# One output store on one DMA ring in place of two stores on two rings, at the end of a load-bound decode kernel

## The chip, the cores and the metric

The kernel runs on one core of a Trainium2 chip. The metric is the device time of one execution in microseconds (us). Most executions agree within 0.3%. Beside the time, a profile gives the span, from the first to the last instruction; the time is about 1.8 us longer than the span.

Engines are called by their names in the profile: PE is TensorE's matmuls and PEld its weight loads, DVE is VectorE, ACT is ScalarE, SP is SyncE. "SPq" and "ACTq" are the sequencers of SyncE and ScalarE where they issue DMA transfers. SyncE's transfers go over queue q1, ScalarE's over q10. In this text such a queue is called a ring.

## The reference

A decode step for 8 sequences: a layer norm, attention of 32 query heads over the last 2,048 positions of a cache with 8 key and value heads, an output projection, and a two-layer perceptron with GELU. Cut to what matters:

```
h  = x + attention(layernorm(x), k_cache[:, :, -2048:], v_cache[:, :, -2048:], wq, wo)
b  = layernorm(h)
x1 = b                      # the token-shift branch is zero for one token
out = h + x1 + gelu(layernorm(x1) @ w3) @ w4        # out: 8 x 1 x 512, bf16
```

The two caches' windows are 67 MB of the 79 MB that must be read. The output is only 8 KB.

## The kernel before

SyncE issues every load: the input, the weights wq, 64 key tiles and 64 value tiles of 512 KB, then wo, w3 and w4. TensorE transposes the keys, does the products, and at the end accumulates the output in one PSUM bank: columns 0 to 255 of the result in partitions 0 to 7, columns 256 to 511 in partitions 32 to 39. The code places the two halves in two column tiles (its tile_position); in the trace of before, the two matmuls of a chunk of w4 start 2 to 6 ns apart.

```
NQ = 2
DQ = D // NQ                                    # 256
out_sb = sb([128, DQ], dt.bfloat16, "out_sb")
fin_ps = b6[:, 0:DQ]                            # fp32, PSUM

W4_CUT = [0, 8, 14]                             # w4 comes in two parts
def sp_prog(e):
    e.dma_start(x_sb[:], A_x...).then_inc(sem_x, 16)
    e.dma_start(wq_v, A_wq...).then_inc(sem_wq, 16)
    # ... 64 key tiles, 64 value tiles, wo, w3, w4: all issued here ...
    store_out(e, 0)
    e.wait_ge(sem_out, 16 * NQ)

def store_out(e, j):
    e.wait_ge(sem_dveP, DVEP_OUT_READY)
    e.dma_start(out.rearrange("b s d -> (b s) d")[:, j * DQ:(j + 1) * DQ],
                out_sb[32 * j:32 * j + B, :]).then_inc(sem_out, 16)

def pe_fin(e):
    # ... residual first, then, for each of the 14 chunks fc of w4 and j in 0, 1:
    #     waits for the part of w4 that fc begins
    #     fin_ps[32*j : 32*j+8, :] += gT[:, chunk fc]^T @ w4_sb[:, fc, half j]

def dve_final(e):
    e.wait_ge(sem_peP, PEP_FIN)
    e.tensor_copy(out_sb[0:40, :], fin_ps[0:40, :]).then_inc(sem_dveP, 1)   # 32*(NQ-1)+B = 40

AC.append(lambda e: store_out(e, 1))            # ScalarE issues the second half
```

Of the kernel before, what the change touches and what calls it, by code (L numbers as in the profile page):

```python
# [6 lines left out]
dt = mybir.dt  # L7
ACT = mybir.ActivationFunctionType
# [3 lines left out]
B = 8  # L12
D = 512
# [20 lines left out]
def bass_sequential_preLN__sliding_block_cached__mixer_s_mlp__decode_kernel(  # L34
# [23 lines left out]
    with es:  # L58
        sb = lambda shape, dtype, name: es.enter_context(nc.sbuf_tensor(name, shape, dtype))
# [69 lines left out]
        gT = sb([128, FC * B], dt.bfloat16, "gT")  # L129
        NQ = 2  # L130
        DQ = D // NQ
        out_sb = sb([128, DQ], dt.bfloat16, "out_sb")

        kT_ps = [ps_t([128, W], dt.bfloat16, f"kT_ps{i}") for i in range(2)]
        S_ps = ps_t([128, 2, 512], dt.float32, "S_ps")
# [16 lines left out]
        sem_out = S("sem_out")  # L152
# [27 lines left out]
        sem_peP = S("sem_peP")  # L180
        sem_dveP = S("sem_dveP")
        sem_actP = S("sem_actP")
# [19 lines left out]
        ev_act = Ev(sem_actP)  # L202
# [26 lines left out]
        def sp_prog(e):  # L229
            e.dma_start(x_sb[:], A_x.rearrange("b s d -> (b s) d")).then_inc(sem_x, 16)  # L230
            e.dma_start(wq_v, A_wq.rearrange("(p k) n -> p k n", k=KC)).then_inc(sem_wq, 16)  # L231
            v_next = 0

            def issue_v(i):
                b, g = divmod(i, G)
                vs = i % NV
                if i >= NV:
                    e.wait_ge(sem_PV, (i - NV) // G + 1)
                e.dma_start(  # L239
                    vnat[:, vs, :].rearrange("p (c d) -> p c d", c=NC),  # L240
                    A_v_cache[b, g, W0:SK, :].rearrange("(p c) d -> p c d", c=NC),
                ).then_inc(sem_v[vs], 16)

            for i in range(NITEM):
                b, g = divmod(i, G)
                ks = i % NK
                if i >= NK:
                    e.wait_ge(sem_Thi, i - NK + 1)
                e.dma_start(  # L249
                    knat[:, ks, :].rearrange("p (c d) -> p c d", c=NC),  # L250
                    A_k_cache[b, g, W0:SK, :].rearrange("(p c) d -> p c d", c=NC),
                ).then_inc(sem_k[ks], 16)
                while v_next <= i - VD and v_next < V_DEFER_FROM:
                    issue_v(v_next)
                    v_next += 1

            def issue_wo(j):
                h0, h1 = WO_CUT[j], WO_CUT[j + 1]
                e.dma_start(wo_v[:, h0:h1, :],  # L259
                            A_wo[h0 * 128:h1 * 128, :].rearrange(  # L260
                                "(h p) n -> p h n", p=128)).then_inc(sem_wo[j], 16)

            e.wait_ge(sem_dveP, DVEP_QBLK)
            wo_next = 0
            while v_next < NITEM:
                if NITEM - v_next == G // 2:
                    while wo_next < WO_EARLY:
                        issue_wo(wo_next)
                        wo_next += 1
                issue_v(v_next)  # L270
                v_next += 1
            while wo_next < WO_PARTS:
                issue_wo(wo_next)
                wo_next += 1
            if W34_LAST_ITEM >= 0:
                e.wait_ge(sem_Thi, W34_LAST_ITEM + 1)
            e.dma_start(w3_sb, B_w3.rearrange("(k p) f -> p k f", k=KC)).then_inc(sem_w3, 16)  # L277
            w4_rows = B_w4.rearrange("(c p j) n -> p c (j n)", p=128, j=2)
            w4_dst = w4_sb.rearrange("p (c j) n -> p c (j n)", j=2)
            for i in range(W4_PARTS):  # L280
                c0, c1 = W4_CUT[i] // 2, W4_CUT[i + 1] // 2
                e.dma_start(w4_dst[:, c0:c1, :], w4_rows[:, c0:c1, :]).then_inc(sem_w4[i], 16)
            store_out(e, 0)
            e.wait_ge(sem_out, 16 * NQ)

        def store_out(e, j):
            e.wait_ge(sem_dveP, DVEP_OUT_READY)
            e.dma_start(out.rearrange("b s d -> (b s) d")[:, j * DQ:(j + 1) * DQ],
                        out_sb[32 * j:32 * j + B, :]).then_inc(sem_out, 16)

        PE, AC, DV = [], [], []

# [286 lines left out]
        fin_ps = b6[:, 0:DQ]  # L579
# [96 lines left out]
        PEP_FIN = ev_pe.next()  # L676
# [22 lines left out]

        def dve_final(e):  # L700
            e.wait_ge(sem_peP, PEP_FIN)
            e.tensor_copy(out_sb[0:32 * (NQ - 1) + B, :], fin_ps[0:32 * (NQ - 1) + B, :]).then_inc(sem_dveP, 1)  # L702
        DV.append(dve_final)

        AC.append(lambda e: store_out(e, 1))

        with nc.Block() as block:
            block.gpsimd(pool_prog)
            block.sync(sp_prog)

            @block.tensor
            def _(e):
                for f in PE:
                    f(e)

            @block.scalar
            def _(e):
                for f in AC:
                    f(e)

            @block.vector
            def _(e):
                for f in DV:
                    f(e)
# [28 lines left out]
```

## Time and profile before

| | before |
|---|---|
| time, median of 4 runs | 207.62 us (207.40 to 207.75) |
| time and span of the profiled run | 207.02 us, 205.2 us |
| bytes over the DMA queues | 79.59 MB, 388 GB/s on average |
| last matmul's end to end of span | 2.3 us, 1.1% of the span |

The first two parts of the profile page of the kernel before follow: busy time, then tenths of busy time in 40 equal slices of the span. PEclk is the granted TensorE clock in tenths of full speed.

```profile
PE 159.2 (78%) x2744; PEld 122.6 (60%) x2744; DVE 83.5 (41%) x197; ACT 81.4 (40%) x100; POOL 3.0 (1%) x13
...
PE   1039975999599967995799878797998698875745
...
PEclk9999999797979799979995998599859797675557
DMA  6999999999999999999999999999999999999980
```

The DMA row is at nine tenths or more in all but the first slice and the last two. The load stream is what lasts; PE is busy for 78% but rarely in a full row. The chain of waits of the same kernel, by engine, says so too:

```profile
DMA 53%; SPq 31%; PE 13%; issue 2%; DVE 0%
```

VectorE has 0% of that chain and ScalarE nothing. Now the end, in the timeline of the kernel before. Columns: start in us, duration in us, engine, line, operation, output and inputs, and in brackets the idle time before it.

```profile
200.06 2.85 PE L692 MATMUL b<-knat,gT 128*8 128x256 bf16 x28 [0.51 <-DMA knat<-in_B_w_dram]
201.89 0.73 PEld L692 LDWEIGHTS b<-knat,gT 128*8 128x8 bf16 x12 [0.46 <-DMA knat<-in_B_w_dram]
202.96 0.42 DVE L702 CAST out_sb<-b 40x256 bf16<-40x256 f32 x1 [5.85 <-PE b L692]
203.40 0.32 SPq L288 DMA_DIRECT2D out_dram<-out_sb  x1
203.41 0.65 ACTq L288 DMA_DIRECT2D out_dram<-out_sb  x1
```

The last group of matmuls waits 0.51 us for the first part of w4, then runs without a gap. One copy of 0.42 us follows, then two issues that start together: SyncE's takes 0.32 us, ScalarE's 0.65 us. What SyncE waits for at the end of the kernel before:

```profile
SPq L707 <- DMA out_dram<-out_sb: 1.1, 1, 1.1
SPq L707 <- PEq L707: 0.2, 1, 0.2
```

That is 1.1 us for the stores to land and 0.2 us for the closing barrier. When the stores' packets move is seen in the DMA view cut to windows. Columns: packets, MB, share of the window on 16 engines. First 203.9 to 204.3 us, then 204.3 to 204.5 us of the kernel before:

```profile
q1 hardware_dynamic: 16, 0.00, 4.5%
...
q10 hardware_dynamic: 16, 0.00, 9.0%
```

SyncE's 16 packets (8 rows of 512 bytes, and 8 of 4 bytes, which stand for the updates of the semaphore) are all over before the first of ScalarE's 16 starts.

### The profile page before, as it was taken

Reading aid. Unit: us, or ns where it says so; the run is one execution under the profiler, and the core shown is the slowest. Engines: PE = TensorE matmul, PEld = TensorE weight load, DVE = VectorE, ACT = ScalarE, POOL = GpSimd, SP = SyncE. Lnnn points to the kernel's source line nnn. Section 1 sums busy time; section 2 is a strip of 40 time slices with the busy share of each in tenths; the row PEclk is TensorE's granted clock in tenths of the full one; section 3 lists DMA queues with packets and bytes.
Section 4 is the critical chain, followed back from the end, with each engine's and each line's share of the span. In section 5 each row is a group of like instructions: output and inputs, shape, how many; then the busy total and the mean of one; then the engine's idle time right before and its main releaser. Section 6 shows DMA issues by size and latency. Waiting matters only on the chain.

```text
span 205.2 us, 6281 instructions
## 1 busy us (share of the span) xinstructions
PE 159.2 (78%) x2744; PEld 122.6 (60%) x2744; DVE 83.5 (41%) x197; ACT 81.4 (40%) x100; POOL 3.0 (1%) x13
## 2 busy tenths in 40 slices
PE   1039975999599967995799878797998698875745
PEld 0039853697469654963487648574876476554632
DVE  5103544544453446343543554346435353352130
ACT  3203656515541554153513551176135431350040
POOL 5000000000000000000000000000000000000000
PEclk9999999797979799979995998599859797675557
DMA  6999999999999999999999999999999999999980
GB/s 206 434 398 415 409 407 409 407 411 408 403 410 406 408 410 410 406 406 410 409 410 405 409 411 410 407 406 410 406 409 408 407 410 385 359 394 328 394 334 28
DMA packets 24266, 79.59 MB, mean 388 GB/s; under 512 B 2200, under 2 KB 6320, under 8 KB 24112
## 3 DMA queue, kind: packets, MB, share of 16 engines
q1 hardware_dynamic: 24224, 79.19, 98.1%
q8 instruction: 22, 0.36, 0.7%
q14 instruction: 4, 0.03, 0.0%
q10 hardware_dynamic: 16, 0.00, 0.0%
HBM read 79.18 MB, written 0.01 MB: 386 GB/s over the span
## 4 chain that ended last, share of the span: by engine, by line
DMA 53%; SPq 31%; PE 13%; issue 2%; DVE 0%
DMA knat<-in_A_k_cache_dram 47%; SPq L239 17%; SPq L249 9%; PE kT_ps L388 6%; DMA knat<-in_B_w_dram 6%; SPq L259 4%; PE misc L526 3%; PE b L692 1%; PE S_ps L418 1%; SPq L277 1%; PE b L507 0%; DVE out_sb L702 0%; SPq L230 0%; SPq L231 0%; PE b L473 0%
## 5 line engine op out<-in xcount | busy, mean ns | idle before, releaser
L388 PE MATMUL kT_ps<-ident_b,knat 128*128 128x128 bf16 x1024 | 83.8, 248 | 21.7 <-DMA knat<-in_A_k_cache_dram 20.8
L399 ACT ACTIVATE kT_sb<-kT_ps 128x1024 bf16<-128x1024 bf16 x64 | 65.4, 1022 | 87.0 <-PE kT_ps L388 87.0
L388 PEld LDWEIGHTS kT_ps<-ident_b,knat 128*128 128x128 bf16 x1024 | 71.8, 113 | 38.6 <-DMA knat<-in_A_k_cache_dram 30.3
L406 DVE COPY kT_sb<-kT_ps 128x1024 bf16<-128x1024 bf16 x64 | 44.2, 691 | 62.8 <-PE kT_ps L388 62.8
L526 PE MATMUL misc<-pT_sb,vnat 128*128 128x4 bf16 x1024 | 29.0, 165 | 3.0 <-issue 1.4
L526 PEld LDWEIGHTS misc<-pT_sb,vnat 128*128 128x128 bf16 x1024 | 27.5, 98 | 6.1 <-issue 3.2
L418 PE MATMUL S_ps<-kT_sb,qblk 128*32 128x512 bf16 x256 | 29.0, 440 | 0.0
L418 PEld LDWEIGHTS S_ps<-kT_sb,qblk 128*32 128x32 bf16 x256 | 6.7, 94 | 9.0 <-issue 3.2
L439 ACT ACTIVATE P_sb<-S_ps,negmcol 128x512 bf16<-128x512 f32 x8 | 5.5, 687 | 7.7 <-DVE negmcol L431 7.6
L360 PE MATMUL S_ps<-xlnT,wbig 128*128 128x8 bf16 x128 | 3.6, 168 | 6.3 <-DMA wbig<-in_A_wq_dram 6.3
L536 DVE TENSOR_TENSOR prod_sb<-misc,w_sb 128x128 f32<-128x128 f32 x8 | 2.3, 292 | 14.6 <-PE misc L526 14.6
L512 DVE COPY w_sb<-b 128x128 f32<-128x128 f32 x8 | 2.3, 292 | 13.2 <-PE b L507 13.2
L360 PEld LDWEIGHTS S_ps<-xlnT,wbig 128*128 128x128 bf16 x128 | 3.5, 104 | 6.4 <-issue 6.4
L429 DVE TENSOR_REDUCE mcol<-S_ps 128x1 f32<-128x512 f32 x8 | 5.5, 682 | 0.6 <-PE S_ps L418 0.6
L584 ACT ACTIVATE std<-var,eps_t 128x8 f32<-128x8 f32 x1 | 0.3, 301 | 12.5 <-DVE var L635 12.5
L376 DVE TENSOR_SCALAR qblk<-S_ps 128x32 bf16<-128x32 f32 x8 | 0.9, 181 | 9.7 <-PE S_ps L360 9.7
L463 ACT ACTIVATE a_row<-d_row 1x128 f32<-1x128 f32 x8 | 2.4, 306 | 5.9 <-DVE d_row L456 5.9
L446 PE MATMUL misc<-ident_f,mcol 128*1 128x128 f32 x16 | 3.8, 328 | 1.0 <-DVE negmcol L431 1.0
L507 PE MATMUL b<-w_row,ones_row 1*128 1x128 f32 x16 | 4.2, 343 | 0.0
L602 PE MATMUL S_ps<-oT_all,wbig 128*128 128x8 bf16 x128 | 3.7, 168 | 0.5 <-DMA wbig<-in_A_wo_dram 0.5
L602 PEld LDWEIGHTS S_ps<-oT_all,wbig 128*128 128x128 bf16 x128 | 3.6, 104 | 0.6 <-DMA wbig<-in_A_wo_dram 0.6
L662 PE MATMUL misc<-uT,knat 128*128 128x8 bf16 x56 | 1.7, 168 | 2.7 <-DMA knat<-in_B_w_dram 2.7
(77 smaller groups left out, 68.6 us busy)
## 6 DMA issues: line engine op xcount, KB each, us to landing
knat<-in_A_k_cache_dram SPq DMA_DIRECT2D x64, 512.0 KB, 15.7
vnat<-in_A_v_cache_dram SPq DMA_DIRECT2D x64, 512.0 KB, 15.8
wbig<-in_A_wq_dram SPq DMA_DIRECT2D x1, 4096.0 KB, 12.2
wbig<-in_A_wo_dram SPq DMA_DIRECT2D x1, 2048.0 KB, 20.3
knat<-in_B_w_dram SPq DMA_DIRECT2D x1, 1792.0 KB, 12.1
wbig<-in_A_wo_dram SPq DMA_DIRECT2D x1, 1024.0 KB, 12.4
wbig<-in_A_wo_dram SPq DMA_DIRECT2D x2, 512.0 KB, 11.2
knat<-in_B_w_dram SPq DMA_DIRECT2D x1, 1024.0 KB, 12.6
```

Of the source, the lines that this page charges most:

```text
L239: e.dma_start(vnat[:, vs, :].rearrange("p (c d) -> p c d", c=NC), A_v_cache[b, g, W0:SK, :].rearrange("(p c) d -> p c d", c=NC),).then_inc ...
L249: e.dma_start(knat[:, ks, :].rearrange("p (c d) -> p c d", c=NC), A_k_cache[b, g, W0:SK, :].rearrange("(p c) d -> p c d", c=NC),).then_inc ...
L259: e.dma_start(wo_v[:, h0:h1, :], A_wo[h0 * 128:h1 * 128, :].rearrange("(h p) n -> p h n", p=128)).then_inc(sem_wo[j], 16)
L360: ins = e.matmul(S_ps[:, 0, h * B:(h + 1) * B], wq_v[:, kc, h * DH:(h + 1) * DH], xlnT[:, kc * B:(kc + 1) * B], start=(kc == 0), stop=(kc ...
L388: ins = e.matmul(buf[:, c * 128:(c + 1) * 128], knat[:, ks, c * DH:(c + 1) * DH], ident_b[:, :], is_transpose=True)
L399: e.activation(kT_sb[:, i % NKT, 0:W // 2], kT_ps[i % 2][:, 0:W // 2], ACT.Copy).then_inc(sem_Elo, 1)
L406: e.tensor_copy(kT_sb[:, i % NKT, W // 2:W], kT_ps[i % 2][:, W // 2:W]).then_inc(sem_Ehi, 1)
L418: ins = e.matmul(S_ps[32 * q:32 * (q + 1), b % 2, :], qblk[:, b, g, :], kT_sb[:, i % NKT, 512 * q:512 * (q + 1)], start=(g == 0), stop=(g ...
L429: ins = e.tensor_reduce(mcol[:, j:j + 1], S_ps[:, j, :], AX.X, ALU.max)
L439: e.activation(P_sb[:, j, :], S_ps[:, j, :], ACT.Exp, bias=negmcol[:, j:j + 1], scale=1.0, accum_out=lcol[:, j:j + 1]).then_inc(sem_exp, 1)
L526: ins = e.matmul(misc[:, OT4.start + q * H + R * g:OT4.start + q * H + R * (g + 1)], vnat[:, vs, c * DH:(c + 1) * DH], pT_sb[:, b % 2, c, ...
L602: ins = e.matmul(hT_ps[:, k * B:(k + 1) * B], wo_v[:, h, k * 128:(k + 1) * 128], oT_all[:, h, :], start=False, stop=(h == H - 1), skip_gro ...
```

## The change

The intent was to have every transfer on SyncE's ring, and to store the output once: VectorE copies the first half and ScalarE, at the same time, the second half, both into one tile of 8 rows by 512, which goes out in rows of 1,024 bytes.

```
-        out_sb = sb([128, DQ], dt.bfloat16, "out_sb")
+        out_sb = sb([B, D], dt.bfloat16, "out_sb")
 ...
-            store_out(e, 0)
-            e.wait_ge(sem_out, 16 * NQ)
-
-        def store_out(e, j):
             e.wait_ge(sem_dveP, DVEP_OUT_READY)
-            e.dma_start(out.rearrange("b s d -> (b s) d")[:, j * DQ:(j + 1) * DQ],
-                        out_sb[32 * j:32 * j + B, :]).then_inc(sem_out, 16)
+            e.wait_ge(sem_actP, ACTP_OUT_READY)
+            e.dma_start(out.rearrange("b s d -> (b s) d"), out_sb[:, :]).then_inc(sem_out, 16)
+            e.wait_ge(sem_out, 16)
 ...
-            e.tensor_copy(out_sb[0:32 * (NQ - 1) + B, :], fin_ps[0:32 * (NQ - 1) + B, :]).then_inc(sem_dveP, 1)
+            e.tensor_copy(out_sb[:, 0:DQ], fin_ps[0:B, :]).then_inc(sem_dveP, 1)
 ...
-        AC.append(lambda e: store_out(e, 1))
+        ACTP_OUT_READY = ev_act.next()
+
+        def act_final(e):
+            e.wait_ge(sem_peP, PEP_FIN)
+            e.activation(out_sb[:, DQ:D], fin_ps[32:32 + B, :], ACT.Copy).then_inc(sem_actP, 1)
+        AC.append(act_final)
```

## The prediction

This was written before the changed kernel was built or run.

> **What bounds the kernel.** It streams 79.59 MB (queue table); in the strip of 40 slices the DMA engines are nine tenths busy from the second slice to the 38th, 388 GB/s on average. The chain of waits is 53% DMA, 31% the sync engine's DMA issue, 13% TensorE, and 0% VectorE. The loads bind until the last weights land at about 199.9 us of 205.2.
>
> **What the change touches.** Only the tail. By the timeline of the last microseconds: the last matmul group runs 200.06 to about 202.91; VectorE copies the accumulator (40x256 fp32 to bf16) from 202.96 in 0.42 us; SyncE issues half of the output at 203.40 (0.32 us), ScalarE the other half at 203.41 (0.65 us); SyncE's wait for the output takes 1.1 us, to about 204.8; the closing barrier ends the span. All that the change can shorten is 203.0 to 205.2: 2.2 us, 1.1% of the span, and most of that (issue, latency, landing, barrier) stays.
>
> **Removed, added, moved.**
> - VectorE's copy keeps its 256 elements per partition; 8 partitions in place of 40 should still take 0.42 us.
> - Added: a ScalarE copy of 8x256. Estimate from ScalarE's groups: 112 columns from PSUM took 264 ns, 1,024 columns 1,022 ns, about 0.83 ns a column, so 256 take about 0.38 us, beside VectorE's: no new time, if both may read the bank at once. They read partitions 0-7 and 32-39, different quadrants, which the Trainium skill, "PSUM — Partial Sum Buffer", section "PSUM bank collisions raise a hardware error", says may be read at the same time; no run shows it yet. No new table load: the trace has 5, none on the line of ScalarE's copies, which alternate with Exp and follow Sqrt.
> - Removed: ScalarE's store. In the DMA view SyncE's packets moved from 204.16 to about 204.31, ScalarE's from 204.29 to about 204.43. So ScalarE's 0.65 us issue costs only the 0.12 us by which its packets end later.
> - The single store has the same 8 rows, of 1,024 bytes in place of 512: no visible cost.
> - Added: one more semaphore wait on SyncE, met or nearly so: about 0.03 us (estimate from gaps of 0.02 to 0.05 us between a release and the next start).
> - Loads, their order and ring, and all earlier instructions stay: nothing before 202.9 us should move.
> - Outside the span (the profiled run took 207.02 us, its span 205.2) lie 1.8 us that the profile does not show. The Trainium skill, "Runtime: NRT & Kernel Launch", section "The launch sequence", lists a reset of DMA rings among the work after a kernel; that one ring fewer shortens it no run shows. I allow 0.1 us.
>
> **Sum.** -0.12 for later packets, +0.03 for the wait, -0.1 outside: -0.2 us. Predicted 207.4 us, range 206.6 to 208.1. Faster by over 2% (4.2 us, more than the whole tail) 2%; within 2% 97%; slower 1%.
>
> **What would show it.** Right: the second output queue is gone; ScalarE's copy takes 0.35 to 0.42 us and starts within 0.05 us of VectorE's; one issue of 0.3 to 0.4 us; an output wait of 0.9 to 1.1 us; last matmul to end of span falls from 2.3 us to 2.0 to 2.25; strip and DMA rate as before; no sixth table load. Wrong: a table load of 1.28 us before ScalarE's copy; the two copies one after the other; a later end of the loads.
>
> **What would make the prediction wrong.** A cost of the second ring over the whole run or outside the span that is bigger than I allow; a table load; a shift in the load stream, where 0.3% would hide all that is computed above.

## The result, and the profile after

| | before | after |
|---|---|---|
| time, median of 4 runs | 207.62 us (207.40 to 207.75) | 207.51 us (207.38 to 207.65) |
| ratio, 95% interval | | 0.9996 (0.9979 to 1.0013) |
| time and span of the profiled run | 207.02, 205.2 us | 207.38, 205.6 us |
| start of the copy, to the end of the span | 202.96 us, 2.28 us | 203.44 us, 2.16 us |

A ratio is the mean time of one kernel's fast runs over that of the other's in the same rounds, so it is not quite the ratio of the medians. Before and after are the same within the spread. The profiled run of after even has the longer span, by 0.36 us. The last row says where the two traces differ and in which direction: the copy starts 0.48 us later, and from there to the end it takes 0.12 us less (the ends, unrounded in the traces, are 205.24 and 205.60 us).

The strips and the chain by engine of the changed kernel's page:

```profile
PEclk9999997975997599769696969579969588885556
DMA  6999999999999999999999999999999999999980
...
DMA 54%; SPq 24%; PE 18%; issue 2%; DVE 0%
```

The load stream is as it was (387 GB/s). The shares of SPq and PE in the chain moved by 7 and 5 points though no load was changed: neither the time nor the DMA strip moved with them, so they are no cost that came or went. The end, in the timeline of the changed kernel:

```profile
200.12 3.28 PE L689 MATMUL b<-knat,gT 128*8 128x256 bf16 x28 [0.50 <-DMA knat<-in_B_w_dram]
201.95 0.95 PEld L689 LDWEIGHTS b<-knat,gT 128*8 128x8 bf16 x12 [0.46 <-DMA knat<-in_B_w_dram]
203.44 0.38 ACT L706 ACTIVATE out_sb<-b 8x256 bf16<-8x256 f32 x1 [4.04 <-PE b L689]
203.44 0.41 DVE L699 CAST out_sb<-b 8x256 bf16<-8x256 f32 x1 [6.27 <-PE b L689]
203.88 0.32 SPq L285 DMA_DIRECT2D out_dram<-out_sb  x1
```

The two copies start together and take 0.38 and 0.41 us; there is no table load before ScalarE's; one issue is left. SyncE's waits of the changed kernel:

```profile
SPq L709 <- DMA out_dram<-out_sb: 1.0, 1, 1.0
SPq L709 <- PEq L709: 0.2, 1, 0.2
```

The first line of the timeline is where the longer span comes from. The same 28 matmuls, which the change does not touch, took 3.28 us after and 2.85 us before. The view of windows shows why. Columns: window, its length, busy time of each engine with its number of instructions, then granted clock, DMA share, GB/s. First the kernel before:

```profile
200.00:202.30 2.30, 2.24 (x22) 1.19 (x24) 0.00 (x0) 0.00 (x0) 0.00 (x0) 0.50 0.16 63
202.30:202.90 0.60, 0.60 (x10) 0.28 (x6) 0.00 (x0) 0.00 (x0) 0.00 (x0) 0.97 0.00 0
```

and the changed kernel:

```profile
200.00:202.30 2.30, 2.18 (x20) 1.17 (x22) 0.00 (x0) 0.00 (x0) 0.00 (x0) 0.50 0.19 71
202.30:202.90 0.60, 0.60 (x10) 0.40 (x6) 0.00 (x0) 0.00 (x0) 0.00 (x0) 0.50 0.00 0
202.90:203.40 0.50, 0.50 (x6) 0.00 (x0) 0.00 (x0) 0.00 (x0) 0.00 (x0) 0.50 0.00 0
```

Both run at half the full clock at first. In the trace of before the granted clock rose to 0.97 for the last 0.6 us; in that of after it stayed at 0.50 to the end. In ten further traces with this group unchanged (the seven kernels of repeated tails, the changed kernel run again, ring_idle and x_on_act, below) it took 3.03 to 3.28 us, so the 2.85 us of the one trace of before is the exception; that trace also came from a quick run of the kernel before (207.02 us; most others were 207.3 to 207.8 us). A difference of 0.43 us between two single traces here is not the change's.

### The profile page after: what moved, and what is told of

Its sections match the earlier page's. It is cut to its first block, busy times and chain, and to the rows that moved or that the text cites. A ratio compares the mean times of both kernels' runs of the same rounds, so it can differ in the third digit from the quotient of the medians.

```text
span 205.6 us, 6282 instructions
## 1 busy us (share of the span) xinstructions
PE 161.1 (78%) x2744; PEld 123.5 (60%) x2744; DVE 83.4 (41%) x197; ACT 81.8 (40%) x101; POOL 3.0 (1%) x13
## 4 chain that ended last, share of the span: by engine, by line
DMA 54%; SPq 24%; PE 18%; issue 2%; DVE 0%
DMA knat<-in_A_k_cache_dram 48%; SPq L239 12%; PE kT_ps L385 10%; SPq L249 7%; DMA knat<-in_B_w_dram 6%; SPq L259 4%; PE misc L523 3%; PE S_ps L415 2%; PE b L689 2%; SPq L277 1%; PE b L470 0%; PE misc L443 0%; PE b L504 0%; PE misc L475 0%; DVE out_sb L699 0%
## 5 line engine op out<-in xcount | busy, mean ns | idle before, releaser
L504 PE MATMUL b<-w_row,ones_row 1*128 1x128 f32 x16 | 4.7, 385 | 0.0
```

## The experiments

A tenth of a microsecond in 207 cannot be read from the time of one run. So the main experiment repeats the tail: in each kernel whose name begins with t17 the tail is done 17 times, each copy waiting until the stores of the one before have landed. The result stays right, since the same numbers are written again, and every microsecond of difference between two such kernels is 17 times that of one tail.

**Theory A**, that of the prediction: the change saves about 0.1 us, because ScalarE's packets come last, and nothing else. **Rival B**: ScalarE's long issue (0.65 us against 0.32) counted in full. **Rival C**: the landing of a store sets all, and nothing is saved. **Rival D**: a second ring costs something in itself, perhaps outside the span.

### t17_two_rings: the tail of before, 17 times

```
-            store_out(e, 0)
-            e.wait_ge(sem_out, 16 * NQ)
+            for r in range(REP):                       # REP = 17
+                store_out(e, 0, r)                     # waits for copy r
+            e.wait_ge(sem_out, 16 * NQ * REP)
 ...
+            for r in range(REP):
+                if r > 0:
+                    e.wait_ge(sem_out, 16 * NQ * r)
                 e.tensor_copy(out_sb[0:40, :], fin_ps[0:40, :]).then_inc(sem_dveP, 1)
 ...
-        AC.append(lambda e: store_out(e, 1))
+        AC.append(lambda e: [store_out(e, 1, r) for r in range(REP)])
```

> The kernel before with its tail (copy, two stores on two rings, wait for both) done 17 times one after the other, each copy waiting until the stores of the one before have landed; the result is the same. From the trace of before one tail lasts about 1.86 us from the start of the copy (202.96) to the landing (about 204.8), with a wake-up about 1.9 us. So 16 more add 30 us: 238 us. This is the yardstick for the three others; all theories agree on it within 2 us.

Measured: 237.50 us (237.41 to 237.61, 4 runs), against 207.60 us of before in the same rounds: 29.9 us for 16 more tails, 1.87 us each, as expected.

### t17_gather: the changed tail, 17 times

The same repetition of the changed kernel's two copies and one store.

> The changed kernel's tail (copies on VectorE and ScalarE side by side, one store) done 17 times in the same way. Theory A (only the later packets of the second ring are saved, less a wait): 0.09 us less a tail than two_rings, so 1.0 to 2.0 us less in all, about 236.5 us. Rival B (ScalarE's issue counts in full, 0.65 us against SyncE's 0.32): 0.33 us less a tail, 5.3 us less, 232.7 us. Rival C (the landing of one store sets it all, nothing is saved): within 0.4 us of two_rings.

Measured: 235.45 us (235.32 to 235.72), 2.05 us less than t17_two_rings, 0.12 us a tail. This is just above the top of theory A's range and far from rivals B (5.3) and C (0). So the change does save something, 0.12 us a tail, which is as much as the single tails of the two traces differ by (2.28 and 2.16 us).

Where do the 0.12 us lie? The timelines show one tail each. t17_two_rings:

```profile
225.95 0.42 DVE L707 CAST out_sb<-b 40x256 bf16<-40x256 f32 x1 [1.45 <-DMA out_dram<-out_sb]
226.39 0.28 SPq L290 DMA_DIRECT2D out_dram<-out_sb  x1
226.39 0.28 ACTq L290 DMA_DIRECT2D out_dram<-out_sb  x1
227.81 0.42 DVE L707 CAST out_sb<-b 40x256 bf16<-40x256 f32 x1 [1.45 <-DMA out_dram<-out_sb]
```

t17_gather:

```profile
226.05 0.38 ACT L714 ACTIVATE out_sb<-b 8x256 bf16<-8x256 f32 x1 [1.37 <-DMA out_dram<-out_sb]
226.05 0.41 DVE L704 CAST out_sb<-b 8x256 bf16<-8x256 f32 x1 [1.33 <-DMA out_dram<-out_sb]
226.50 0.28 SPq L287 DMA_DIRECT2D out_dram<-out_sb  x1
227.80 0.37 ACT L714 ACTIVATE out_sb<-b 8x256 bf16<-8x256 f32 x1 [1.38 <-DMA out_dram<-out_sb]
```

From copy to copy it is 1.86 and 1.75 us. ScalarE's issue of 0.65 us was a cost of the first time only; from the second tail on it takes 0.28 us as SyncE's does (the median over the 17 is 0.28 us). The first tail, which has the long issue as the kernel before has, is no exception: from its copy to the second it is 1.90 us with two rings and 1.77 us with one store, 0.13 us apart. From the issue to the next copy it is 1.42 us with two rings and 1.30 us with one store. The packets' own records in the traces divide this further; the values are medians over 17 tails, counted from the first packet:

| | first packet after issue | last packet's end after first packet | last packet's end to next copy |
|---|---|---|---|
| t17_two_rings | 0.76 us | 0.184 us (SyncE's 0.093, then ScalarE's) | about 0.48 us |
| t17_gather | 0.76 us | 0.169 us | about 0.37 us |

The third column is what remains of the period after copy, issue and packets. This contradicts a part of theory A. The single store's data packets of 1,024 bytes took 52 ns each (median) where those of 512 bytes took 25 ns, and so the single store's packets ended only 0.015 us before the second ring's. The other 0.10 to 0.11 us lie between the last packet and the moment at which the waiting engine goes on. The packed traces narrow this further, for they hold the moment of each update of the output's semaphore (no view prints them). In both kernels the next copy starts 0.02 us after the last update. So the engine's waking is not what differs: the last update itself comes 0.45 us after the last packet with two rings and 0.35 us with one store.

### t17_two_on_sp: both stores on SyncE's ring

```
             for r in range(REP):
                 store_out(e, 0, r)
+                store_out(e, 1, r)
 ...
-        AC.append(lambda e: [store_out(e, 1, r) for r in range(REP)])
```

> As two_rings, but both stores are issued by SyncE, one after the other: one ring without the gathering. Theory A: the second issue of 0.32 us starts after the first, its packets come about 0.33 us after the first's where the second ring's came 0.12 us after; 0.2 us more a tail, 3.2 us more than two_rings, about 241 us. If a second ring in itself costs something (rival D), this is faster than two_rings.

Measured: 239.72 us (239.55 to 240.00), 2.2 us more than t17_two_rings, 0.13 us a tail. Theory A had 0.2. "One ring" alone is thus a loss; the second issue follows the first on one sequencer, and the packets end 0.43 us after the first packet, 0.25 us later than with two rings. But from the last packet to the next copy it is 0.37 us, as in t17_gather, and not 0.48. So 0.10 us of the 0.25 is won back there: the two rings pay 0.1 us after the last packet, and two stores on one ring do not.

### t17_vector_only: one store, both copies by VectorE

```
                 e.tensor_copy(out_sb[:, 0:DQ], fin_ps[0:B, :])
+                e.tensor_copy(out_sb[:, DQ:D], fin_ps[32:32 + B, :]).then_inc(sem_dveP, 1)
 ...
-        AC.append(act_final)          # and SyncE's wait for it
```

> As gather, but VectorE makes both copies one after the other and ScalarE none. Theory A: the second copy adds 0.35 to 0.4 us a tail, so 5.6 to 6.5 us more than gather, about 242.5 us, and more than two_rings: the gathering pays only because ScalarE's copy runs beside VectorE's. If reading one bank at once slowed the two copies in gather, the difference would be smaller than 0.3 us a tail.

Measured: 242.72 us (242.36 to 243.22), 7.27 us more than t17_gather, 0.43 us a tail. A second copy of 0.42 us counts in full (one odd tail in the trace, 0.43 us longer than the others for a reason not looked into, can make up the rest). This bears on whether reading one bank from two engines at once slows them:

```profile
L714 ACT ACTIVATE out_sb<-b x17: 374/374/375, 203.3 to 231.3; 8x256 bf16<-8x256 f32 x17
L704 DVE CAST out_sb<-b x17: 411/412/413, 203.3 to 231.3; 8x256 bf16<-8x256 f32 x17
...
```

These are the copies in t17_gather, with minimum, median and maximum in ns. VectorE's is 412 ns beside ScalarE's; in t17_vector_only, with no ScalarE at work, the same copy has a median of 412 ns as well. Reading the two quadrants (partitions 0 to 7 and 32 to 39) at the same time costs VectorE's copy nothing; ScalarE's copy was not timed without VectorE's beside it. Without ScalarE the gathering would be a loss of 0.31 us a tail against the kernel before (242.72 less 237.50, over 17).

### ring_idle: the second ring in use, but not in the tail

```
             chain(e, ins, "act_self", act_self)        # after ScalarE's warm-up
+            e.dma_start(x_again[:], A_x...).then_inc(sem_again, 16)
 ...
+            e.wait_ge(sem_again, 16)                   # before ScalarE's last copy
```

> The changed kernel, and ScalarE loads the 8 KB input a second time into a tile that nobody reads, right after its warm-up: the second ring is in use again, but not in the tail. Theory A (a second ring costs nothing in itself, inside the span or outside): time within 0.3 us of the kernel before and of the changed kernel, 207.3 to 207.8 us, and time less span 1.75 to 1.9 us as in both. Rival D (a second ring costs setting up or resetting outside the span, which the change saves): time less span larger than 1.9 us, and the time above the kernel before.

Measured: 207.55 us (207.37 to 207.62, 5 runs), ratio to before 1.0001 (0.9989 to 1.0014). Time less span was 1.75 to 1.93 us in its runs, 1.76 to 1.93 us in those of before in the same rounds, and 1.75 to 1.88 us in those of after. The spans are on record to 0.1 us, so the means say more: over all rounds 1.81 us in the 30 runs of before and ring_idle, and 1.81 us in the 9 runs of the change. The added wait had a small cost of its own: in the trace ScalarE's copy starts 0.06 us after VectorE's, and from the copies to the end it is 2.22 us in place of 2.16. Rival D falls as far as this resolves: outside the span a second ring costs nothing that can be seen, and the time of the whole is the same within 0.3 us.

### t17_gather_act and t17_two_on_act: ScalarE's ring alone

The delay of 0.1 us after the last packet may belong to ScalarE's ring (theory R) or to two rings being at work at once (theory P). In t17_gather_act ScalarE issues the single store; in t17_two_on_act ScalarE issues both stores of before.

```
# t17_gather_act
-    SyncE:   wait for both copies; e.dma_start(out, out_sb)
+    ScalarE: e.activation(...); wait for both copies; e.dma_start(out, out_sb)
# t17_two_on_act
-        AC.append(lambda e: [store_out(e, 1, r) for r in range(REP)])
+        AC.append(lambda e: [store_out(e, j, r) for r in range(REP) for j in range(2)])
```

> The 17 gathered tails, but the one store of each is issued by ScalarE (the second ring) instead of SyncE. Why: in the seventeen tails the saving was 0.12 us, but the packets of the single store end only about 0.015 us sooner after the first packet than the last of the two rings' (0.169 against 0.184 us); the rest, about 0.10 us, lies between the last packet and the next copy's start (0.37 us with one store by SyncE, 0.38 with both stores by SyncE, 0.48 with two rings). Theory R (a store on ScalarE's ring lands 0.1 us later than one on SyncE's): 1.6 us more than the gathered tails, about 237.1 us. Theory P (ScalarE's ring is as fast when it is alone, the 0.1 us comes from two rings at work at once): within 0.5 us of 235.45 us.

> The tail of before 17 times, both stores issued by ScalarE one after the other: the second ring alone. Theory R: 1.6 us more than both on SyncE, about 241.3 us, and about 0.48 us from the last packet to the next copy. Theory P: about 239.7 us and 0.38 us.

Measured: t17_gather_act 235.71 us (235.21 to 236.02), 0.26 us more than t17_gather in the earlier rounds, in which before took 207.60 us as against 207.61 us here. t17_two_on_act 240.42 us (240.39 to 240.51), 0.70 us more than t17_two_on_sp, of which 0.23 us lie in the first tail: there ScalarE's first issue took 0.58 us and the second had to wait for it, so that the first period is 2.31 us (2.06 in t17_two_on_sp). The periods between tails (medians, from copy to copy) are 1.769 against 1.745 us and 2.033 against 2.005 us. One tail of t17_gather_act, then the copies of t17_two_on_sp and of t17_two_on_act; in brackets is VectorE's idle time, which was 1.45 us in t17_two_rings and 1.33 us in t17_gather:

```profile
226.48 0.37 ACT L710 ACTIVATE out_sb<-b 8x256 bf16<-8x256 f32 x1 [1.40 <-DMA out_dram<-out_sb]
226.48 0.41 DVE L700 CAST out_sb<-b 8x256 bf16<-8x256 f32 x1 [1.36 <-DMA out_dram<-out_sb]
226.94 0.28 ACTq L713 DMA_DIRECT2D out_dram<-out_sb  x1
...
227.37 0.42 DVE L708 CAST out_sb<-b 40x256 bf16<-40x256 f32 x1 [1.59 <-DMA out_dram<-out_sb]
...
226.03 0.42 DVE L707 CAST out_sb<-b 40x256 bf16<-40x256 f32 x1 [1.62 <-DMA out_dram<-out_sb]
```

So ScalarE's ring alone is slower by 0.02 to 0.03 us a tail, not by 0.1. Theory R falls; theory P stands: most of the delay is there only when stores of both rings are in flight together. The semaphore's updates say which store pays. SyncE's store has its last update 0.34 to 0.35 us after its last packet in every kernel of repeated tails that has one (medians). ScalarE's has it 0.35 us after when its ring is alone, and 0.45 us after (0.44 in t17_split_two_rings, next) when SyncE's store goes out beside it.

What in it makes the delay was not settled. In the two-ring tails the last packets of the two stores end 0.09 us apart; with both stores on one ring they are 0.34 us apart. So it may be the nearness of two completions and not the two rings as such. Nor was it tried with a semaphore for each store: in all these kernels both stores count on one. No run separates these. The mere number of updates is not the cause, since two stores on one ring have as many.

### t17_split_two_rings: the copies of the change, the stores of before

```
-                e.wait_ge(sem_actP, ACTP_OUT_READY + r)
-                e.dma_start(out..., out_sb[:, :])
+    SyncE:      e.dma_start(out...[:, 0:DQ], out_sb[:, 0:DQ])       # after VectorE's copy
+    ScalarE:    e.dma_start(out...[:, DQ:D], out_sb[:, DQ:D])       # after both copies
```

> The gathered tile with VectorE's and ScalarE's copies as in the change, but two stores of 512 bytes a row, SyncE's after VectorE's copy, ScalarE's after both copies. Both theories of the second ring: as two_rings, 237.2 to 237.8 us, since copies of 8 rows beside one another take as long as one of 40 rows. If the saving came from the smaller copy and not from the stores, it is at 235.5 us like the gathered tails.

Measured: 237.27 us (236.90 to 237.42), 0.23 us less than t17_two_rings and 1.8 us more than t17_gather. The saving is in the stores, not in the copies.

### after_again: the change itself in 5 rounds

> The change itself once more, in 5 rounds. By the seventeen tails it should be 0.12 us faster than before, ratio 0.9994, on top of a spread of the fast runs of 0.3 us or more that comes from elsewhere (the clock granted in the last matmuls alone was worth 0.4 us between the two profiles). So 207.3 to 207.6 us, and the interval of the ratio will very likely include 1.

Measured: 207.42 us (207.26 to 207.51, 5 runs) against 207.61 us (207.32 to 207.68, 9 runs), ratio 0.9992 (0.9979 to 1.0004). The median is 0.19 us lower, and the interval includes 1, as was expected. In its trace the last matmuls took 3.27 us and the span from the copy's start to the end was 2.16 us, as in the first trace of after.

### x_on_act, w4_fine, x_and_w4: where a second ring and smaller parts do help

The traces pointed to two things near the critical path. The load stream begins behind the issue of the 8 KB input (0.74 us; the first big load follows at 1.19 us). And TensorE waits 0.5 us for the first part of w4 before its last group. x_on_act gives the input's load to ScalarE, w4_fine cuts w4 into four parts, x_and_w4 does both. All keep the change.

```
# x_on_act
 def sp_prog(e):
-    e.dma_start(x_sb[:], A_x...).then_inc(sem_x, 16)
 def act_warm(e):
+    e.dma_start(x_sb[:], A_x...).then_inc(sem_x, 16)
# w4_fine
-        W4_CUT = [0, 8, 14]
+        W4_CUT = [0, 4, 8, 12, 14]              # and four semaphores
```

> The changed kernel, with the 8 KB load of the input issued by ScalarE instead of SyncE, as its first instruction: the second ring is used where it takes an issue out of SyncE's queue ahead of the load stream. In the trace the first big load is issued at 1.19 us, 0.44 us after the input's. If the stream's start sets its end: 0.3 to 0.5 us less than the changed kernel, 207.1 us, ratio to before about 0.997. If buffers or the bandwidth in between absorb the earlier start: within 0.15 us of the changed kernel. ScalarE's table load and the first normalisation may come later by 0.4 us; the projection waits 6.5 us for its weights, so that costs nothing.

> The changed kernel, with the last weights in four parts (4, 4, 4 and 2 of 14 chunks) in place of two (8 and 6). In both traces TensorE stands 0.5 us between the end of the residual's matmuls (199.6) and the landing of the first part, and is then busy without a gap at half clock until the copies. With the first part half as big it can start 0.5 us sooner and the rest lands in time: 0.3 to 0.6 us less than the changed kernel, copies at about 202.9 us, ratio about 0.997. If the later parts land later because of the extra issues, or the stream's own variation is larger: within 0.2 us.

> Both together. If the two are independent (one at the start of the stream, one behind its end): 0.7 to 1.0 us less than the changed kernel, about 206.6 us, ratio to before about 0.995: beats both kernels clear of noise. If one absorbs the other, only 0.3 to 0.5 us less.

| | median, 5 runs | ratio to before, 95% interval |
|---|---|---|
| x_on_act | 206.88 us (206.84 to 207.06) | 0.9973 (0.9960 to 0.9985) |
| w4_fine | 206.88 us (206.70 to 206.93) | 0.9969 (0.9956 to 0.9981) |
| x_and_w4 | 206.51 us (206.21 to 206.68) | 0.9950 (0.9936 to 0.9963) |

All came out as expected: within 2%, but with intervals clear of 1. (The expectation of w4_fine says that both traces end at half clock. That holds for the changed kernel; in the trace of before the clock rose for the last 0.6 us, as shown above.) The ratios, taken of 207.6 us, are 0.56, 0.64 and 1.04 us less than before; without the 0.12 us of the change itself that leaves 0.44 us for the input's load, 0.52 us for the parts of w4 and 0.92 us for both, so the two gains add up. The timeline of x_and_w4 shows both. The issues at the start, first in the changed kernel, then in x_and_w4:

```profile
0.74 0.39 SPq L230 DMA_DIRECT2D x_sb<-in_A_x_dram  x1
1.19 0.37 SPq L231 DMA_DIRECT2D wbig<-in_A_wq_dram  x1
...
0.73 0.59 ACTq L290 DMA_DIRECT2D x_sb<-in_A_x_dram  x1
0.74 0.41 SPq L230 DMA_DIRECT2D wbig<-in_A_wq_dram  x1
```

and the last matmuls and copies of x_and_w4:

```profile
199.17 3.26 PE L689 MATMUL b<-knat,gT 128*8 128x256 bf16 x28
...
202.47 0.37 ACT L706 ACTIVATE out_sb<-b 8x256 bf16<-8x256 f32 x1 [3.36 <-PE b L689]
202.47 0.41 DVE L699 CAST out_sb<-b 8x256 bf16<-8x256 f32 x1 [5.57 <-PE b L689]
```

The big load goes out at 0.74 us in place of 1.19. The last group starts at 199.17 us, with no wait of its own, in place of 200.12, and the copies at 202.47 in place of 203.44 us. x_and_w4 is the best version: it beats both kernels.

## Why the prediction was right

It said 207.4 us, 206.6 to 208.1, and "within 2%" at 97%; measured were 207.51 and, again, 207.42 us.

- **The bound of the argument held.** All that the change touches lies after the last matmul: 2.3 us of 205.2. Even without all of it, 2% (4.2 us) could not have been reached.
- **The loads did not move.** The DMA strip is the same digit for digit, at 387 against 388 GB/s.
- **ScalarE's copy costs no time.** The estimate was 0.38 us from its other groups; measured 0.375 us, beginning with VectorE's, and VectorE's copy unchanged at 0.41 us. No table load was added. The Trainium skill's statement ("PSUM — Partial Sum Buffer", section "PSUM bank collisions raise a hardware error") that two engines may read different quadrants of a bank at once agrees with these runs: the results are right, and VectorE's copy takes 412 ns with ScalarE's beside it and without.
- **"-0.12 for later packets": right in size, wrong in its account.** The tails show 0.12 us saved. But the packets end only 0.015 us sooner in the repeated tails (0.03 us in the two single traces: 0.169 against 0.196 us), because packets of 1,024 bytes take twice as long; "no visible cost" of the longer rows was wrong. About 0.1 us is saved in another place, between the last packet and the last update of the semaphore, where two rings at once are slower than one. That the two errors cancelled was luck.
- **"+0.03 for the wait": less than 0.01 us.** From the end of VectorE's copy to SyncE's issue it is 0.027 us with two rings and 0.034 us with the gathered tile (medians over the tails; the two single traces have 0.028 and 0.034).
- **"-0.1 outside": not there.** Time less span is 1.74 to 1.93 us in the runs of before and of ring_idle, which use the second ring, and 1.73 to 1.92 us in those of the change, which does not, with means of 1.81 us in both. No run shows that the reset of rings which the Trainium skill lists ("Runtime: NRT & Kernel Launch", section "The launch sequence") depends on it.
- **The sum.** -0.2 us was predicted; the tails say -0.12 us, the two direct comparisons -0.04% and -0.08%, which is -0.1 to -0.2 us, with intervals that include zero. The repeated tails, not the direct comparison, show that the saving exists. The predicted range, 1.5 us wide, is over ten times the effect: that the time fell into it confirms the bound, and none of the three terms.

The profile of one run would have misled: its span rose by 0.36 us, because the clock granted in the last matmuls differed by more than the change is worth.

## What to carry to other kernels

Bound a change first by the stretch that it can touch; here that alone (1.1% of the span) fixed the answer. If an effect is smaller than the spread of runs, repeat it in a chain within one kernel, where each repetition waits for the one before, and divide; single traces differ by more for other reasons, such as the granted clock. A second DMA ring is worth using where it takes an issue out of the way of the stream that bounds the kernel, as the input's load at the start does (0.44 us here); for two small stores at the end, gathering them into one is a little better, provided that the gathering runs on an engine that is idle anyway.

## What the Trainium skill lacked or had wrong

- "DMA: Bandwidth & Descriptors", section "Issuing engines are not separate DMA queues", says that issuing from several engines only saves the sequencers' issue time. Here two 4 KB stores on two rings were 0.13 us a tail faster than on one ring, but 0.1 us of the gain was lost between the last packet and the waiting engine's start (0.48 against 0.37 us). The page lacks such a loss; its cause is open.
- The same page, "Specifications", gives a first-byte latency of about 0.6 us for SyncE's and ScalarE's path. From the start of an issue to the first packet it was 0.76 us here (median of the repeated tails), with all other traffic over; this may count from another point. The issue of a DMA on ScalarE took 0.57 to 0.65 us the first time and 0.28 to 0.31 us (medians) after that; neither that section nor the one named above tells of it.
- "ScalarE: Activation LUTs", section "What ACT_TABLE_LOAD costs", gives 186 ns and 0.833 ns a column for an ACTIVATE with immediate scale and bias, 399 ns for 256 columns. The copy of 8x256 from PSUM took 374 to 375 ns.
